# A recurrent cell's sigmoids, one to a batch, set behind the next step's decay copy, with some PSUM copies given to VectorE

## The chip, the cores and the metric

One core of a Trainium2 chip runs the kernel. Its engines work side by side, each on its own list of instructions: TensorE (PE; PEld is its weight loads), VectorE (DVE), ScalarE (ACT), GpSimd (POOL), and SyncE (SP), which here only issues transfers. Each engine takes its instructions in program order. The metric is the time of one execution on the device, in microseconds.

## The reference

Two blocks in a row. The first is a gated recurrence over 768 time steps, for 4 batches, 8 heads and a head width of 40; the second sends each of the 3072 resulting rows of 320 through one of 8 two-layer networks, chosen from a token number.

```python
for t in range(S):
    m_new = np.maximum(f_gate[:, :, t] + m, i_gate[:, :, t])
    f_stab = np.exp(f_gate[:, :, t] + m - m_new)
    i_stab = np.exp(i_gate[:, :, t] - m_new)
    C = f_stab * C + i_stab * (vt outer kt)
    n = f_stab * n + i_stab * kt
    h_tilde = C @ qt
    denom = np.maximum(np.abs(n . qt), 1.0)
    o = 1.0 / (1.0 + np.exp(-o_gate[:, :, t]))
    y[:, :, t] = o * h_tilde / denom
...
expert_idx = token_ids * 2654435761 % E
out[mask] = np.maximum(xe @ w1[e], 0.0) @ w2[e]
```

What the change is about is the line `o = ...`: a sigmoid over all elements of `o_gate`, 768 x 8 x 40 for each batch.

## The kernel before

**Stages.** The first stage (up to about 160 us of the profile) computes the recurrence in blocks of 128 time steps, as masked attention inside a block and a state `C` of 40 x 41 numbers per head carried from block to block. There are 6 blocks in a batch (`NB`), 4 batches, so 24 steps `s`, with `b = s // 6` and `c = s % 6`. The second stage gathers rows by expert and runs the networks on TensorE. All is Float32 with some BF16 helpers. The program order is written out by hand (`tc.manual_schedule()`): what a function issues goes to the end of each engine's list, and semaphores are put in where one engine reads what another wrote, or reuses a buffer.

**One step of the first stage**, in the order in which it is issued (L760 to L827):

- transfers for later steps on SP's queue (k, v, q, gate `og`, expert weights);
- `decayed` (L375): POOL multiplies the state by the decay `dec` copied in the step before;
- `turn_k` (L283): TensorE transposes k of step s+2, 128x512, into PSUM, and ScalarE copies it to `kT` (L289);
- `turn_q` (L295): the same for a block of q of the next batch, copied to `qT` (L302). For batches 1 to 3 the q rows are loaded six to a partition, so a block's columns are written with a step of 6 elements (`slice(r, None, NB)`);
- `back` and `finish` (L443, L451): the finished block of a batch before is transposed to `xo` in PSUM, VectorE forms the denominator `den`, multiplies by the gate `og`, POOL divides, and SP stores the rows;
- `decays` (L316): TensorE forms the log-decays `ab` of step s+1 in two halves, ScalarE takes their exponential into `w` (L328);
- in steps 3, 9 and 15, `load_e`: a transfer on ScalarE's queue (L203);
- in steps 5, 11 and 18, the sigmoids (L800), on `og` in place, 128x1920 for a batch;
- `state` (L386): TensorE forms k'v into the PSUM tile `ht`, VectorE adds it to the state `C`;
- `entering` (L330): for a step s+1 that is not the first of its batch, TensorE forms `xb`, VectorE multiplies it into `qs` (L340), and ScalarE copies the last column to `dec` (L342), the decay copy;
- `load_a` on SP, `k_weights` (L344) on POOL, and the stores of the finished rows on SP;
- `scores` (L359) of step s+1 on TensorE, then `weigh` (L370): VectorE multiplies the scores into `w` (L373, two instructions);
- `pad_q` (L291): VectorE spreads the q rows that the next step transposes; then in most steps some work of the routing tables (L648 to L655), on VectorE and POOL;
- `attend` (L404): TensorE forms the step's output in `ht`, and ScalarE copies it to `hB` (batches 0 to 2) or `hT` (batch 3) (L439);
- in steps 13 to 20, `route_table` (L623): a product on TensorE and two sums on VectorE (L631, L632).

**Buffers.** The PSUM tiles `tr`, `xo`, `ab`, `xb` and `tk` share one ring of four (`tag="tr", bufs=4`): each new one waits until the one four before it has been read. `ht` is a single buffer. `og` has three, so batch 3 takes the one of batch 0.

**ScalarE's tables.** Exponential and sigmoid need different tables; each change between them puts a load (ACT_TABLE_LOAD) into ScalarE's list, in front of the first instruction that needs it. Copies run with either.

**The place of the sigmoids.** Batch 0's is issued in step 5, those of batches 1 and 2 one after the other in step 11, batch 3's in step 18, each behind the exponentials of `decays(s + 1)` and ahead of `entering(s + 1)`. For steps 5 and 11 the next step is the first of a batch, so `entering` issues nothing there.

Of the kernel before, what the change touches and what calls it, by code (L numbers as in the profile page):

```python
# [17 lines left out]
P = 128  # L18
# [4 lines left out]
def kernel(  # L23
# [24 lines left out]
    nc = tc.nc  # L48
    B, H, S, D = q.shape
    BH = B * H  # L50
    NB = S // P
# [53 lines left out]
    def weight_slices(e):  # L105

        W[e], slices = weights(moe_w1[e], moe_w2[e], wpools[e % 3 > 0], w2pools[e % 6 > 0])
        return slices
# [8 lines left out]
    with tc.tile_pool(name="gates", bufs=1) as gp, \  # L117
# [35 lines left out]
        qb = {}  # L153
# [5 lines left out]
        def load_k(s):  # L159
            st[s] = {"k": ks[s % NK], "v": vs[s % NK]}  # L160
            nc.sync.dma_start(ks[s % NK][:, :, :D], rows_of(k, s))

        def load_v(s):
            nc.sync.dma_start(vs[s % NK][:, :, :D], rows_of(v, s))
# [5 lines left out]
        LB = B - 1  # L170

        def load_o(b, part):
            if part == 0:
                og[b] = ld.tile([P, H, NB * D], F32, name="og", bufs=3)
            if b == LB:
                nc.sync.dma_start(gate(b, part), rows_of(o_gate, b * NB + part))
                return
            hs = slice(part * PR, (part + 1) * PR)
            nc.sync.dma_start(og[b][:, hs], o_gate[b, hs].rearrange("h (p r) d -> p h (r d)", r=NB))
# [6 lines left out]
        def load_q(b, part):  # L186

            if part == 0:
                qb[b] = {"l": ld.tile([P, H, NB * D], F32, name="ql", bufs=2)}
            hs = slice(part * PR, (part + 1) * PR)  # L190
            nc.sync.dma_start(qb[b]["l"][:, hs], q[b, hs].rearrange("h (p r) d -> p h (r d)", r=NB))
# [80 lines left out]
        def gates_turn(rows):  # L272
# [7 lines left out]
                kw_T[:, :, lo:hi_, :].rearrange("p c g n -> p c (g n)"), tp[:],  # L280
            )

        def turn_k(s):  # L283
            d = st[s]
            d["kT"] = wk.tile([P, PR, P], F32, name="kT")
            tp = ps.tile([P, PR, P], F32, name="tr", tag="tr", bufs=4)
            for j in range(PR):
                nc.tensor.transpose(tp[:, j, :], d["k"][:, 2 * j : 2 * j + 2, :].rearrange("p h d -> p (h d)"), ident[:])
            nc.scalar.copy(d["kT"][:], tp[:])  # L289

        def pad_q(b, r):  # L291
            t = qb[b][r] = qps[(2 + r) % 4]
            nc.vector.tensor_copy(t[:, :, :D], qb[b]["l"][:, :, r * D : (r + 1) * D])

        def turn_q(b, r, cols):  # L295
            if "T" not in qb[b]:
                qb[b]["T"] = wk.tile([P, PR, S], F32, name="qT")
            t = qb[b].pop(r)
            tp = ps.tile([P, PR, P], F32, name="tr", tag="tr", bufs=4)
            for j in range(PR):  # L300
                nc.tensor.transpose(tp[:, j, :], t[:, 2 * j : 2 * j + 2, :].rearrange("p h d -> p (h d)"), ident[:])  # L301
            nc.scalar.copy(qb[b]["T"][:, :, cols], tp[:])  # L302


        def load_q0(c):
            t = qb.setdefault(0, {})[c] = qps[c % 2]
            nc.sync.dma_start(t[:, :, :D], rows_of(q, c))

        def turn_q0(c):
            turn_q(0, c, slice(c * P, (c + 1) * P))  # L310
# [33 lines left out]
        def k_weights(s):  # L344
            b, c = s // NB, s % NB
            d = st[s]
            if c + 1 < NB:
                d["kw"] = kws[s % 2]
                nc.gpsimd.tensor_tensor(
                    d["kw"][:, :, :D], d["k"][:, :, :D],  # L350
                    kw_T[:, c % 2, c // 2, b * H : (b + 1) * H].unsqueeze(2).to_broadcast([P, H, D]), op=ALU.mult,
                )
# [3 lines left out]
        def sigmoid(b):  # L356
            nc.scalar.activation(og[b][:], og[b][:], AF.Sigmoid)
# [17 lines left out]
        def decayed(s):  # L375
            c = s % NB
            if c == 0:
                st["C"] = None
            if c + 1 < NB:
                st["Cn"] = Cs[s % 2]  # L380
                if c > 0:
                    nc.gpsimd.tensor_tensor(
                        st["Cn"][:, :, :D1], st["C"][:, :, :D1], st[s]["dec"][:].to_broadcast([P, PR, D1]), op=ALU.mult,
                    )
# [19 lines left out]
        def attend(s):  # L404

            c = s % NB
            d = st[s]

            def place(j, hf):
                return d["ht"][j % 2 * DP : (j % 2 + 1) * DP, hf, j // 2 * P : (j // 2 + 1) * P]  # L410

            if c > 0:
                for j in range(PR):
                    for hf in range(2):
                        r = slice(hf * DP, (hf + 1) * DP)
                        nc.tensor.matmul(
                            place(j, hf), lhsT=st["C"][r, j, :], rhs=d["qs"][r, j, :],
                            start=(j < 2), stop=False, skip_group_check=True,
                        )
            for j0 in range(0, PR, 2):  # L420
                for hf in range(2):
                    for j in (j0, j0 + 1):
                        nc.tensor.matmul(  # L423
                            place(j, hf), lhsT=d["v"][:, 2 * j + hf, :], rhs=d["w"][:, hf, j, :],
                            start=(c == 0 and j0 == 0), stop=True,
                            skip_group_check=True,
                        )
            if c + 1 < NB:
                st["C"] = st["Cn"]
            b = s // NB  # L430
            if b == LB:
                hT[b, c] = wk.tile([P, 2, 2, P], F32, name="hT")[:]
                to = hT[b, c]
            else:
                if c == 0:
                    hB[b] = wk.tile([P, 2, 2, S], F32, name="hB")
                hT[b, c] = hB[b][:, :, :, c::NB]
                to = hB[b][:, :, :, c * P : (c + 1) * P]
            nc.scalar.copy(to, d["ht"][:, :, : 2 * P].rearrange("p f (i t) -> p f i t", t=P))  # L439

        hB, hT = {}, {}

# [317 lines left out]
        for s in range(NT):  # L760
            b, c = s // NB, s % NB
            if 0 < s < NT - 3:
                load_k(s + 3)
                if b == 0 and c < 3:
                    load_q0(c + 3)
            if s + 3 < NT:
                load_v(s + 3)
            if c in (2, 4) and b + 2 < B:
                load_q(b + 2, c // 2 - 1)
            for bo, part in o_loads.get(s, ()):  # L770
                load_o(bo, part)
            if s < 2:
                load_q(1, s)
            if s == NB + 4:
                slices += weight_slices(0)
            if slices:
                slices.pop(0)()
            decayed(s)
            if s + 2 < NT:
                turn_k(s + 2)  # L780
            if b == 0 and c < 4:
                turn_q0(c + 2)
            if b + 1 < B:
                for r in (turns_of if b else first_turns).get(c, ()):
                    turn_q(b + 1, r, slice(r, None, NB))
            done = [(b - 1, c)] if b > 0 else []
            if b == LB and c > 0:
                done.append((b, c - 1))
            stores = [finish(*br, back(*br)) for br in done]
            if s == 0:  # L790
                spin(5)
            if s + 1 < NT:
                decays(s + 1)
            if s == 0:
                store_a(g1, A)
                store_e(g1, A)
                store_e(g0, nc.sync)
            if c == 3 and b + 1 < B:
                load_e(b + 1, [0, 1, 2])
            for bo in {NB - 1: (0,), 2 * NB - 1: (1, 2), 3 * NB: (LB,)}.get(s, ()):  # L800
                sigmoid(bo)
            state(s)
            if s + 1 < NT:
                entering(s + 1)
                if 0 < s < NT - 2:
                    load_a(s + 2, nc.sync)
                if s == 0:
                    A.activation(aP[g1], aP[g1], AF.Exp)
                    load_a(2, A)
                    load_e(0, [1, 2])  # L810
                k_weights(s + 1)
            for store in stores:
                store()
            if s + 1 < NT:
                scores(s + 1)
                weigh(s + 1)
            nb = b + (c == NB - 1)
            if nb + 1 < B and s + 1 < NT:
                for r in (turns_of if nb else first_turns).get((c + 1) % NB, ()):
                    pad_q(nb + 1, r)  # L820
            for do in before.get(s, []):
                do()
            attend(s)
            if s == 0:
                gates_turn(g1)
            for do in after.get(s, []):
                do()  # L827
# [255 lines left out]
    with tc.manual_schedule():  # L1083
# [55 lines left out]
        for e in range(E):  # L1139
            g, i = e // EG, e % EG  # L1140
# [94 lines left out]
```

## Time and profile before

| | |
|---|---|
| median of 4 runs (lowest to highest) | 409.27 us (408.74 to 410.97) |
| the profiled execution: its time | 408.99 us |
| the profiled execution: its span | 407.2 us |
| first stage | until about 160 us |
| sigmoid, L357, 4 instructions | 7.1 us, 1802 ns each |
| table loads for sigmoid, L357, 3 | 1283 ns each |
| table loads for exponential behind them, L328, 3 | 1283 ns each |
| copies L439 (hB, hT), ACT, 24 | 14.0 us, 583 to 586 ns each |
| copies L289 (kT), ACT, 24 | 14.0 us, 585 ns each |
| copies L302 (qT), ACT, 24 | 22.6 us, 976 ns mean, 1099 ns median |
| products L373 (w), DVE, 48 | 30.9 us, 686 ns each |
| products L340 (qs), DVE, 20 | 13.6 us, 680 ns each |

The span runs from the first to the last instruction that the profiler shows; the execution's time has some 1.8 us around it. Times in a timeline are microseconds from the span's start: first the start of an instruction or a run of equal ones, then its length, engine, line, operation, tiles (written <- read), shapes, and in brackets the idle time ahead of it on its engine with what ended it. In the list of waits the numbers are total us, count, and the longest.

### The profile page before, as it was taken

What the parts mean: (1) busy time and instruction counts of PE and PEld (TensorE: products, weight loads), DVE (VectorE), ACT (ScalarE), POOL (GpSimd) and SP (SyncE); (2) the same over time, 40 slices, a digit from 0 to 9 for tenths busy, and PEclk for the clock granted to TensorE, in tenths of its full rate; (3) what the DMA queues carried; (4) which work ended last, traced back from release to release, by engine and by line L of the source; (5) the groups of instructions that cost most, each with busy time, mean ns of one, the idle gap of its engine ahead of it and who ended that gap; (6) DMA issues with size and microseconds to landing.
All of it is one profiled execution on the core that took longest, in us unless ns stands there. A gap on an engine that the chain in (4) does not pass through costs nothing. (4 is left out here: it accounts for less than half of the span.)

```text
span 407.2 us, 8799 instructions
## 1 busy us (share of the span) xinstructions
PE 382.2 (94%) x3406; PEld 313.5 (77%) x3406; DVE 213.5 (52%) x515; ACT 150.2 (37%) x290; POOL 200.6 (49%) x253
## 2 busy tenths in 40 slices
PE   8689989997999998999999999999999999999991
PEld 7568767875887775556998988977989989889771
DVE  7656647774786774235246347354345463452500
ACT  6334797579557541011114232241231141321300
POOL 6653103323544641784296395692592883907011
PEclk9959999999999999999999999999999999999998
DMA  7587856986678512447958137244236201000001
GB/s 143 110 191 160 209 110 153 238 200 132 150 170 184 143 48 81 104 165 224 336 205 257 66 99 225 82 113 147 88 106 183 81 2 47 2 15 34 0 17 35
DMA packets 96166, 51.47 MB, mean 126 GB/s; under 512 B 68022, under 2 KB 90170, under 8 KB 96122
## 3 DMA queue, kind: packets, MB, share of 16 engines
q1 hardware_dynamic: 88330, 36.65, 36.5%
q0 software_dynamic: 2496, 8.20, 6.3%
q10 hardware_dynamic: 5296, 6.03, 4.7%
q8 instruction: 28, 0.46, 0.5%
q14 instruction: 16, 0.13, 0.1%
HBM read 41.98 MB, written 8.63 MB: 124 GB/s over the span
## 5 line engine op out<-in xcount | busy, mean ns | idle before, releaser
L846 POOL DMA_INDIRECT out_dram<-zo,s_idx x26 | 27.2, 1046 | 89.7 <-DVE zo L1076 52.4
L465 POOL TENSOR_TENSOR x<-x,den 128x320 f32<-128x320 f32 x23 | 16.6, 722 | 50.7 <-DVE den L463 25.1
L373 DVE TENSOR_TENSOR w<-sp,w 128x512 f32<-128x512 f32 x48 | 30.9, 686 | 14.6 <-PE sp L365 12.9
L1038 PE MATMUL zp<-w2t,h 128*128 128x320 f32 x128 | 36.5, 438 | 0.0
L365 PE MATMUL sp<-qT,kT 64*128 64x128 f32 x384 | 29.4, 291 | 3.1 <-ACT qT L302 1.6
L1038 PEld LDWEIGHTS zp<-w2t,h 128*128 128x128 f32 x128 | 23.3, 190 | 11.4 <-issue 2.1
L365 PEld LDWEIGHTS sp<-qT,kT 64*128 64x128 f32 x384 | 24.6, 193 | 9.6 <-issue 4.5
L1008 ACT ACTIVATE h<-h 128x832 f32<-128x832 f32 x14 | 12.6, 897 | 47.6 <-DVE h L1007 47.6
L836 POOL DMA_INDIRECT xg<-x_rows,g_idx x24 | 23.3, 971 | 12.4 <-issue 12.4
L1048 PE MATMUL zp<-t,s 128*128 128x160 f32 x192 | 27.7, 300 | 1.3 <-DVE s L1033 0.6
L328 ACT ACTIVATE w<-ab 128x512 f32<-128x512 f32 x48 | 26.7, 611 | 5.8 <-PE ab L324 5.7
L1048 PEld LDWEIGHTS zp<-t,s 128*128 128x128 f32 x192 | 26.5, 190 | 1.7 <-ACT p L1062 0.9
L423 PE MATMUL ht<-w,v 128*64 128x128 f32 x384 | 27.1, 285 | 0.0
L1022 POOL TENSOR_TENSOR t<-w2t,t 128x640 f32<-128x640 f32 x16 | 24.7, 1543 | 0.6
L956 PE MATMUL mb<-xs,ws 128*128 128x208 f32 x112 | 25.0, 346 | 0.0
L1022 POOL TENSOR_TENSOR t<-w2t 128x640 f32<-128x640 f32 x16 | 24.8, 1551 | 0.1
L956 PE MATMUL ma<-xT,w1t 128*128 128x208 f32 x112 | 24.8, 346 | 0.0
L423 PEld LDWEIGHTS ht<-w,v 128*64 128x64 f32 x384 | 21.2, 140 | 4.0 <-issue 3.1
L302 ACT COPY qT<-tr 128x512 f32<-128x512 f32 x24 | 22.6, 976 | 0.8 <-PE tr L301 0.8
L956 PEld LDWEIGHTS mb<-xs,ws 128*128 128x128 f32 x112 | 19.6, 190 | 1.8 <-issue 1.5
L956 PEld LDWEIGHTS ma<-xT,w1t 128*128 128x128 f32 x112 | 18.9, 190 | 1.8 <-issue 1.8
L1048 PE MATMUL zp<-w2t,h 128*128 128x160 f32 x128 | 20.2, 301 | 0.0
(248 smaller groups left out, 864.8 us busy)
## 6 DMA issues: line engine op xcount, KB each, us to landing
w2t<-in_moe_w_dram SPq DMA_DIRECT2D x24, 320.0 KB
w1t<-in_moe_w_dram SPq DMA_DIRECT2D x24, 256.0 KB
k<-in_k_dram SPq DMA_DIRECT2D x24, 160.0 KB
v<-in_v_dram SPq DMA_DIRECT2D x24, 160.0 KB
x_rows<-x SPq DMA_DIRECT2D x24, 160.0 KB
ql<-in_q_dram SPq DMA_DIRECT2D x6, 480.0 KB
og<-in_o_gate_dram SPq DMA_DIRECT2D x6, 480.0 KB
w2t<-in_moe_w_dram ACTq DMA_DIRECT2D x8, 320.0 KB
```

Source lines behind the costliest of these rows:

```text
L302: nc.scalar.copy(qb[b]["T"][:, :, cols], tp[:])
L328: nc.scalar.activation(w[:, hf], ab[:], AF.Exp)
L365: nc.tensor.matmul(sp[hf][:, j, :], lhsT=d["kT"][r, j, :], rhs=q_of(s)[r, j, :], start=True, stop=True,)
L373: nc.vector.tensor_tensor(d["w"][:, hf], d["sp"][hf][:], d["w"][:, hf], op=ALU.mult)
L423: nc.tensor.matmul(place(j, hf), lhsT=d["v"][:, 2 * j + hf, :], rhs=d["w"][:, hf, j, :], start=(c == 0 and j0 == 0), stop=True, skip_group ...
L465: eng.tensor_tensor(xv, xv, den[:].to_broadcast([P, 2, PR, D]), op=ALU.mult)
L836: nc.gpsimd.indirect_dma_start(out=xg, out_offset=None, in_=x_d[:, :], in_offset=bass.IndirectOffsetOnAxis(ap=idx, axis=0),)
L846: ins = nc.gpsimd.indirect_dma_start(out=out[:, :], out_offset=bass.IndirectOffsetOnAxis(ap=idx, axis=0), in_=zo[:], in_offset=None, bound ...
L956: nc.tensor.matmul(dst[:, i, :], lhsT=x(2 * q + i), rhs=y, start=(start and i == 0), stop=stop, skip_group_check=True,)
L1022: nc.gpsimd.tensor_tensor(d[:], x, y[:] if y in (t1, t2) else y, op=ALU.subtract)
L1038: nc.tensor.matmul(zp[:], lhsT=h[:, fb, 2 * P : 3 * P], rhs=w2t[:, fb, :], start=(fb == 0), stop=(fb == FB - 1),)
L1048: nc.tensor.matmul(dst, lhsT=x[:, i], rhs=y[:, i], start=(start and i == 0), stop=(i == FB // 2 - 1), skip_group_check=True,)
```

## The change

The sigmoids are now issued behind `k_weights(s + 1)`, so behind `entering(s + 1)` with its decay copy, and each batch has a step of its own: 5, 11, 15 and 18 for batches 0 to 3. In those steps the copy L439 of `attend` is issued on VectorE in place of ScalarE, and in the steps after them (6, 12, 16, 19) the copies L289 and L302 of `turn_k` and `turn_q`. `turn_k(s)` is called with the step s+2, so it looks up `s - 3`; `turn_q` is given the step and looks up `s - 1`. The calls of `turn_q` for batch 0 keep ScalarE.

```diff
+        sig = {NB - 1: 0, 2 * NB - 1: 1, 2 * NB + 3: 2, 3 * NB: LB}
+
+        def from_psum(s):
+            return nc.vector.tensor_copy if s in sig else nc.scalar.copy
+
         def turn_k(s):
...
-            nc.scalar.copy(d["kT"][:], tp[:])
+            from_psum(s - 3)(d["kT"][:], tp[:])
...
-        def turn_q(b, r, cols):
+        def turn_q(b, r, cols, s=0):
...
-            nc.scalar.copy(qb[b]["T"][:, :, cols], tp[:])
+            from_psum(s - 1)(qb[b]["T"][:, :, cols], tp[:])
...
-            nc.scalar.copy(to, d["ht"][:, :, : 2 * P].rearrange("p f (i t) -> p f i t", t=P))
+            from_psum(s)(to, d["ht"][:, :, : 2 * P].rearrange("p f (i t) -> p f i t", t=P))
...
-                    turn_q(b + 1, r, slice(r, None, NB))
+                    turn_q(b + 1, r, slice(r, None, NB), s)
...
-            for bo in {NB - 1: (0,), 2 * NB - 1: (1, 2), 3 * NB: (LB,)}.get(s, ()):
-                sigmoid(bo)
             state(s)
             if s + 1 < NT:
                 entering(s + 1)
...
                 k_weights(s + 1)
+            if s in sig:
+                sigmoid(sig[s])
             for store in stores:
                 store()
```

## The prediction

> **What bounds the kernel now.** I read the engine shares first, then TensorE's waits, then the timeline around each sigmoid.
>
> ```profile
> span 407.2 us, 8799 instructions
> PE 382.2 (94%) x3406; PEld 313.5 (77%) x3406; DVE 213.5 (52%) x515; ACT 150.2 (37%) x290; POOL 200.6 (49%) x253
> PEclk9959999999999999999999999999999999999998
> ```
>
> TensorE (PE) is busy 94% of the span, at full granted clock from the fourth of the 40 slices on, so well before the first sigmoid at 56.8 us. Time can only come from the holes in its work. Its waits by releaser:
>
> ```profile
> PE xo L448 <- ACT hB L439: 3.1, 2, 2.4
> ...
> PE sp L365 <- ACT qT L302: 1.6, 3, 1.2
> ...
> PE xo L448 <- ACT hT L439: 1.4, 2, 0.7
> ...
> PE tr L301 <- DVE qp L293: 0.6, 2, 0.3
> ```
>
> The columns are total us, times, longest. The first row is two waits, 0.69 and 2.38 us, right behind the sigmoids of steps 5 and 11. Of the third, 0.64 us lies behind the sigmoid of step 18; the other, 0.74, is the last block's. The fourth is the two q transposes of the steps after the first two sigmoids. The second has nothing to do with a sigmoid. So what the change can touch is 0.69 + 2.38 + 0.64 + 0.6 = 4.3 us, and that is its ceiling. The timeline of ScalarE (start, length) at the dearest one, step 11, where two sigmoids run together:
>
> ```profile
> 88.89 1.28 ACT L357 ACT_TABLE_LOAD   x1
> 90.19 3.50 ACT L357 ACTIVATE og<-og 128x1920 f32<-128x1920 f32 x2
> 93.59 0.56 ACT L439 COPY hB<-ht 128x512 f32<-128x512 f32 x1
> 94.06 0.59 ACT L289 COPY kT<-tr 128x512 f32<-128x512 f32 x1
> 94.53 1.11 ACT L302 COPY qT<-tr 128x512 f32<-128x512 f32 x1
> 95.66 1.28 ACT L328 ACT_TABLE_LOAD   x1
> ```
>
> TensorE finished the attention output at 90.80, but its copy to hB waits for both sigmoids until 93.59; the transposes xo of step 12 start at 94.21. VectorE is idle meanwhile:
>
> ```profile
> 91.22 0.19 DVE L599 CAST rc<-rc_i 128x48 f32<-128x48 int32 x1
> 95.13 0.17 DVE L454 TENSOR_SCALAR den<-xo 128x8 f32<-128x8 f32 x1 [3.72 <-PE xo L448]
> ...
> 96.31 0.68 DVE L340 TENSOR_TENSOR qs<-qT,xb 128x512 f32<-128x512 f32 x1
> 97.58 1.29 DVE L373 TENSOR_TENSOR w<-sp,w 128x512 f32<-128x512 f32 x2 [0.59 <-ACT w L328]
> ```
>
> Behind the attention stage TensorE never waits 1 us, and the gathers, spins and weight loads there hang on the last step; what is won or lost before 160 us arrives at the end whole.
>
> **The change, part by part.** Steps 5, 11, 15 and 18 carry one sigmoid each; in each, the copy hB or hT (L439), and in the next step the copies kT (L289) and qT (L302; none in step 19), go from ScalarE to VectorE: 4 + 4 + 3 copies. Step 15 is new; its sigmoid costs one more pair of table loads.
>
> Durations. ScalarE: load 1.28, sigmoid 1.80, from the rows. Copies on VectorE have no row. hB and kT: the PSUM copy of 128x384 (L866) takes 557 ns, that of 128x164 (L400) 328 ns, so 1.04 ns an element and 0.69 us for 512, which is also what L340 and L373 take (680, 686). qT writes every sixth float: on ScalarE this raises 0.585 to 1.10 us. Bounds for VectorE: 0.69 (stride free) and 1.47 (the only strided vector row, the reduction L593, 623 ns for 192 elements against 329 ns for 168 in L558: 2.6 ns an element). I take 1.10, ScalarE's own row for this same write. Vector instructions follow each other about 0.08 before the printed end of the one before. A vector result reaches TensorE after 0.11 (pad L293 ends 63.98, load for L301 at 64.09).
>
> The ring matters: "tr" has four PSUM buffers. In a step they go to kT, qT, xo, ab, ab, xb, so the second ab waits for the kT copy and xb for the qT copy.
>
> *Step 11, sigmoid pair split.* VectorE is free at 91.33: hB 91.33 to 92.02, kT to 92.63, qT to 93.65. PE: xo at 92.13 (before 94.21), xb at 93.65 + 0.11 = 93.76 (95.84), scores(13) at 94.09 (96.17). Vector chain: den starts at 93.57, C 0.86 later (the four den instructions back to back, 60.74 to 61.60 in the next paragraph), qs 94.68; scores end at 95.25, weigh starts at 95.34 (97.58). ScalarE: sigmoid ends 91.99, load back 93.28, exponentials behind ab (93.5) in time. Weigh, pad, q transpose: all 2.24 earlier. **-2.24 us.**
>
> *Step 5, same sigmoid, copies moved.* VectorE has routing work until 58.58, so hB runs 58.50 to 59.19, hardly earlier than ScalarE had it (59.04). kT to 59.80, qT to 60.82; xb at 60.93 (60.72), scores 61.25 (61.04), ending 62.41. den starts at 60.74 instead of 59.94, C 61.60, qs 61.85, weigh 62.50 against 62.45, for it waited 0.59 for the exponential before. Pad and q transpose follow: **+0.05.** The stall has changed its owner.
>
> *Step 15, new.* ScalarE has nothing to do from the decay copy to the copy of hB:
>
> ```profile
> 113.74 0.16 ACT L342 COPY dec<-xb 128x4 f32<-128x4 f32 x1 [0.52 <-DVE qs L340]
> ...
> 115.59 0.59 ACT L439 COPY hB<-ht 128x512 f32<-128x512 f32 x1 [1.68 <-PE ht L423]
> ```
>
> Load, sigmoid, load: 113.90 + 1.28 + 1.80 + 1.28 = 118.3, so the next exponentials begin 0.6 later than their 117.69, ready at 119.4 for a weigh at 120.4. That cover holds, even if the load back were held until the first ab is written, at 117.6: exponentials until 120.1. VectorE is what gives: busy 5.71 of 7.40 us between 113.6 and 121, it gets 0.69 + 0.69 + 1.10 more. Its routing one-hot ends 116.23: hB 116.14 to 116.83, the two table sums until 117.18, kT 117.10 to 117.79, qT to 118.81. PE: ab at 117.29 and 117.90 (117.15 and 117.46), xb at 118.92 against 118.04. Scores 0.88 later; C, qs and weigh end at 120.49 against 119.62, 0.87. **+0.88** (qT at 0.69: +0.47; at 1.47: +1.25).
>
> *Step 18.* The decay copy no longer waits for the sigmoid (132.35 becomes 129.83), but nobody needed it sooner: the state product on POOL (L382, 132.83) stands behind other POOL work ending 132.86. hT: 132.13 to 132.82, 0.16 earlier than ScalarE. kT 133.09 to 133.78 now stands ahead of den, so the first xo is read by 134.46 and xb goes at 134.57 against 134.51: **+0.06.**
>
> The sigmoid issues no DMA; batch 3's input-piece load on ScalarE's own queue in step 15 (112.27) stays ahead of it, and nothing is moved on SP's or POOL's queue. The values of batch 2 are read first at 132.79, ready at 117.0.
>
> Sum: 0.05 - 2.24 + 0.88 + 0.06 = **-1.25 us**. With qT at 0.69: -1.7. At 1.47: step 5 +0.37, step 11 -1.9, step 15 +1.25, so -0.2. The profiled execution took 408.99 us (span 407.2), 0.28 under the median of 409.27; I put the difference on the median: **408.0 us**, forecast's own range 407.6 to 409.1.
>
> In the trace a load costs 1283 ns and the sigmoid starts 20 ns after it (88.89 + 1.28, then 90.19); no drain shows. The Trainium skill, "ScalarE: Activation LUTs" (What ACT_TABLE_LOAD costs; Rules for kernel authors), speaks against this change: do all of one set before switching, about 2.66 us a switch, 1.38 of it a drain. By that page step 15 would hold its exponentials until 121.0, weigh would come 1.2 us later still, and the sum would be about -0.1; the rows decide for 1.28.
>
> ScalarE's qT rows (0.585 flat, 1.10 at a step of 24 bytes) show that this write is dear. "SBUF — State Buffer" (the note on cachelines) says lines have 16 bytes and each access to a new line pays, without a price; by that page, if VectorE paid a whole second pass over 512 elements at the rows' 1.04 ns, an estimate of 0.69 + 0.53 = 1.22 us, the sum would be about -1.0.
>
> **The rivals.**
> A, *the stalls vanish whole*: 4.3 us off, 405.0. For it: VectorE idles 3.72 us at step 11. Against: it holds routing work at the three others, and has to take qT there too.
> B, *slower: the vector copies are stretched by GpSimd's work beside them.* The row for it is L1031, 692 ns at best, 1820 at worst, mean 1078 with POOL active: +0.39 an instruction. At that price eleven copies cost 4.2 us, -1.25 + 4.2 = +3.0, 412.2. It makes the kernel slower by 0.5% from 0.30 us a copy on. Against: POOL shows 12.06 us idle before 60.92 and 6.43 before 96.14, exactly where six of the copies fall, and L1031 reads SBUF, the copies PSUM.
> C, *VectorE does not catch up*: step 15's 0.88 is paid a second time in step 17, whose vector load is as high: -1.25 + 0.88 = -0.4, 408.9. Against: it idles 1.25 us a step there (0.68 + 0.37 + 0.20).
>
> **How the numbers follow.** Forecast 0.56, A 0.20, B 0.12, C 0.12. A measurement here can tell about 0.5%, 2.05 us, from no change. Faster by more: A and a little of the forecast's edge, 0.23. Slower by more: most of B, 0.11. Within: 0.66. The range goes from 406.8 (from the forecast's lower edge, 407.6, a third of the way to A) to 409.9 (C with qT at its dear end, 408.9 + 1.05). It leaves out most of B and half of A, 0.2.
>
> **What would show it.** Right: qT on VectorE near 1.1 us, and the times from scores to scores over the four places: 54.59 to 61.04, 88.02 to 96.17, 112.76 to 118.36 and 128.98 to 134.84 before, so 6.45, 8.15, 5.60 and 5.86, become about 6.7, 6.1, 6.5 and 5.9, with the intervals behind them not longer than before. Wrong: a vector copy over 1 us without a stride (B), or a second long interval behind step 16 (C), or a load back that starts only when ab is ready.

## The result, and the profile after

The changed kernel takes 408.3 us at the median (405.51 to 413.73) beside 409.08 us (407.03 to 414.01) for the kernel before, measured in turn on the same chips. The ratio is 0.9978, with a 95% interval of 0.9965 to 0.9992: a gain of 0.9 us, between 0.3 and 1.4. (The ratios leave out the few executions that took over 1.5% longer than the fastest of their kernel; the medians and ranges hold them.) Two more series of the changed kernel, on the chips of the experiments, gave 407.52 beside 409.38 (0.9958, 0.9928 to 0.9989) and 407.73 beside 409.79 (0.9961, 0.9943 to 0.9979). All three lie on the faster side, and all three gains are within what was called too small to tell from no change.

The head of the page of the changed kernel: the span, the busy time of each engine, and the clock that TensorE was granted in each of 40 slices.

```profile
span 406.0 us, 8793 instructions
PE 383.1 (94%) x3406; PEld 314.0 (77%) x3406; DVE 220.0 (54%) x526; ACT 146.6 (36%) x281; POOL 201.1 (50%) x253
PEclk9959999999999999999999999999999999999997
```

VectorE has eleven instructions more, the eleven copies, and 6.5 us more work; ScalarE has eleven copies less and one pair of table loads more. TensorE is as full as before. Its list of waits (total us, count, longest) shows who holds it now:

```profile
PE xo L454 <- DVE hB L445: 1.5, 2, 0.9
...
PE xo L454 <- DVE tv L637: 0.6, 1, 0.6
...
PE ab L330 <- DMA R<-decay_pieces: 0.4, 1, 0.4
...
PE ab L330 <- DVE kT L295: 0.2, 1, 0.2
```

The row of 3.1 us on ScalarE's hB is gone and one of 1.5 us on VectorE's hB stands in its place: the stall of step 5 changed its owner, 0.69 becoming 0.93, and that of step 11 went from 2.38 to 0.57. The second row is step 18, where hT now comes from VectorE (0.64 before, 0.56 now). The last row is new and belongs to step 15. The third is a wait for a transfer, far from any sigmoid; it comes back below. (Lines of the changed kernel are numbered six higher than those of the kernel before.)

The groups of VectorE's copies, with count, busy us and the mean ns of one:

```profile
L308 DVE COPY qT<-tr 128x512 f32<-128x512 f32 x3 | 3.2, 1079 | 0.0
...
L295 DVE COPY kT<-tr 128x512 f32<-128x512 f32 x4 | 2.7, 682 | 0.0
```

The best measure of each place is the time from one step's scores to the next step's on TensorE. The stretch behind a place is added, since a late vector chain can shift work into it. Here and below, the scores, the weigh or the interval of a step are those issued in it; since a step issues the scores of the next block, the scores of step 11 are those of block 12. Some of the recorded expectations count by the block ("the scores of step 12", "step 16") and mean the same instructions.

| place | before | after | difference | predicted |
|---|---|---|---|---|
| step 5 (two intervals) | 6.45 + 5.40 | 6.66 + 5.25 | +0.06 | +0.05 |
| step 11 (two intervals) | 8.15 + 5.39 | 6.41 + 5.25 | -1.88 | -2.24 |
| step 15 | 5.60 | 6.40 | +0.80 | +0.88 |
| step 18 | 5.86 | 5.85 | -0.01 | +0.06 |
| sum | | | -1.03 | -1.25 |

Outside the places, and behind the first three blocks, one more interval differs between these two profiles: from the scores of block 9 to those of block 10 (issued in steps 8 and 9), 5.49 before and 6.14 after, by the wait for the transfer. So the first stage ends only some 0.4 us earlier in the profile after, and the other 0.8 us of the difference between the two spans (407.2 and 406.0) arises behind it, where the two programs are the same: the stretch from the first product zp of the first expert to that of the second takes 27.57 in the one (188.57 to 216.14) and 26.87 in the other (188.13 to 215.00). That the spans differ by 1.2 and the sum was 1.25 is thus partly chance. The table, not the span, is the test of the prediction.

### The profile page after: what moved, and what is told of

Read it like the earlier page. It is cut to its first block, busy times and chain, and to the rows that moved or that the text cites. A ratio compares the mean times of both kernels' runs of the same rounds, so it can differ in the third digit from the quotient of the medians.

```text
span 406.0 us, 8793 instructions
## 1 busy us (share of the span) xinstructions
PE 383.1 (94%) x3406; PEld 314.0 (77%) x3406; DVE 220.0 (54%) x526; ACT 146.6 (36%) x281; POOL 201.1 (50%) x253
## 5 line engine op out<-in xcount | busy, mean ns | idle before, releaser
L1044 PEld LDWEIGHTS zp<-w2t,h 128*128 128x128 f32 x128 | 23.3, 190 | 11.4 <-issue 2.1
L1054 PEld LDWEIGHTS zp<-w2t,h 128*128 128x128 f32 x128 | 18.5, 190 | 2.0 <-issue 1.0
```

The lines of the kernel that those rows point to most:

```text
L1044: nc.tensor.matmul(zp[:], lhsT=h[:, fb, 2 * P : 3 * P], rhs=w2t[:, fb, :], start=(fb == 0), stop=(fb == FB - 1),)
L1054: nc.tensor.matmul(dst, lhsT=x[:, i], rhs=y[:, i], start=(start and i == 0), stop=(i == FB // 2 - 1), skip_group_check=True,)
```

## The experiments

**Sigmoids one to a batch, all copies left on ScalarE.** Which half of the change does the work in step 11, the split of the pair or VectorE's copies?

Against the changed kernel:

```diff
         def from_psum(s):
-            return nc.vector.tensor_copy if s in sig else nc.scalar.copy
+            return nc.scalar.copy
```

> One sigmoid per batch in steps 5, 11, 15, 18 behind the decay copy, all copies left on ScalarE. Theory (VectorE's copies are what makes the fourth sigmoid bearable): step 5 unchanged, step 11 -1.65 us (one sigmoid of 1.80 less ahead of the copies, the exponentials still last), step 15 +1.0 (copies behind the sigmoid, then the load back), step 18 +0.6 (the sigmoid ends 0.6 later than before because the decay copy goes first): sum near 0, ratio 0.999 to 1.001. Rival (the split alone makes the gain): as the changed kernel, ratio 0.998 or below.

Measured: 408.19 us beside 409.38, ratio 0.9977 (0.995 to 1.0004), unclear. The intervals are 6.46 in step 5, 6.46 in step 11 (-1.69), 6.59 in step 15 (+0.99) and 6.53 in step 18 (+0.67): they add up to nothing. The split alone wins nearly what the whole change wins in step 11, and loses it in steps 15 and 18. The median is lower by 1.2 us all the same, so the intervals of one profile do not tell the whole; the hole in step 12 is 0.69 here, and what a long hole does to the clock comes below.

**The pair kept in step 11, VectorE's copies there, and nothing in step 15.** Against the changed kernel:

```diff
-        sig = {NB - 1: 0, 2 * NB - 1: 1, 2 * NB + 3: 2, 3 * NB: LB}
+        sig = {NB - 1: (0,), 2 * NB - 1: (1, 2), 3 * NB: (LB,)}
...
-            if s in sig:
-                sigmoid(sig[s])
+            for bo in sig.get(s, ()):
+                sigmoid(bo)
```

> The two sigmoids of step 11 stay together, nothing in step 15; the copies of steps 5, 11 and 18 (and of the steps behind them) on VectorE. Theory (the copies waiting behind the sigmoids were the stall, not the sigmoids' length): step 5 +0.05, step 11 -2.0 (now held by the exponentials: second sigmoid ends 93.7, load back 95.0, first half 95.6, 0.25 later than VectorE would be ready), step 15 nothing, step 18 +0.06: -1.9 us, ratio 0.9945 to 0.9965, 0.6 to 0.9 us better than the changed kernel. Rival (the split is what pays): the pair keeps the exponentials and so the weighing of step 12 late, step 11 gains under 0.7 us, ratio 0.998 to 1.0.

Measured: 406.81 us beside 409.38, ratio 0.9938 (0.9913 to 0.9963). Step 11 takes 6.42 + 5.24, the same as with the pair split; step 15 is back at 5.60; step 18 is 5.84. ScalarE's timeline of this kernel at step 11 (start, length) and VectorE's beside it:

```profile
89.87 3.50 ACT L363 ACTIVATE og<-og 128x1920 f32<-128x1920 f32 x2
93.39 1.28 ACT L334 ACT_TABLE_LOAD   x1
94.68 1.08 ACT L334 ACTIVATE w<-ab 128x512 f32<-128x512 f32 x2
```

```profile
91.36 0.68 DVE L445 COPY hB<-ht 128x512 f32<-128x512 f32 x1
91.96 0.68 DVE L295 COPY kT<-tr 128x512 f32<-128x512 f32 x1
92.56 1.10 DVE L308 COPY qT<-tr 128x512 f32<-128x512 f32 x1
...
95.38 1.29 DVE L379 TENSOR_TENSOR w<-sp,w 128x512 f32<-128x512 f32 x2 [0.20 <-PE sp L371]
```

With the three copies on VectorE, ScalarE runs both sigmoids until 93.37 and nobody waits: the first of two exponentials that take 1.08 together, from 94.68, is ready for a weigh at 95.38 that the scores release. The split and the copies are two cures for the same stall. Each is enough alone (-1.69 and -1.73 on the interval, -1.74 for both), so the split bought nothing more and cost 0.80 in step 15.

**Old steps and the old pair, only the new place behind the decay copy.** Against the changed kernel (the loop over `sig` as in the experiment before):

```diff
-        sig = {NB - 1: 0, 2 * NB - 1: 1, 2 * NB + 3: 2, 3 * NB: LB}
+        sig = {NB - 1: (0,), 2 * NB - 1: (1, 2), 3 * NB: (LB,)}
...
-            return nc.vector.tensor_copy if s in sig else nc.scalar.copy
+            return nc.scalar.copy
```

> The sigmoids in their old steps, two in step 11, all copies on ScalarE; only their place in the step is the new one, behind the decay copy. For steps 5 and 11 this leaves every engine's order of work as it was. Theory 1 (the wait for a decay piece in the interval of the scores of step 9 to 10, 5.59 to 6.39 us instead of 5.49 in six of six profiles with the new place and routing work in its old one, comes from the new place): above 5.55 again. Rival (it comes and goes with the execution): 5.49. Step 18: the sigmoid ends 0.6 later than before, so the interval behind it is 6.5 instead of 5.86, as in e1_split_only; step 11 keeps its hole, 8.15 or, with a fall of the clock behind it, 8.6 to 9.2. Ratio 1.0005 to 1.004.

Measured: 410.16 us beside 409.11, ratio 1.0034 (0.9993 to 1.0075), unclear. Step 18 takes 6.52 instead of 5.86, as in the first experiment. TensorE's timeline of this kernel at steps 12 and 19:

```profile
93.45 0.81 PE L454 MATMUL xo<-ident,hB 128*128 128x128 f32 x4 [2.38 <-ACT hB L445]
...
96.12 2.02 PE L371 MATMUL sp<-qT,kT 64*128 64x128 f32 x16
```

```profile
134.37 0.65 PE L454 MATMUL xo<-ident,hT 128*128 128x128 f32 x4 [1.30 <-ACT hT L445]
```

The hole of 2.38 us is what it was before: in step 11 there is no decay copy to go behind, so the place changes nothing there. In step 18 the sigmoid now starts later, and a ScalarE copy behind it holds the transposes for 1.30 us, 0.66 more than before. So the new place by itself can only lose, and what makes it free in the changed kernel is VectorE's copy. (The scores of 2.02 us, elsewhere 1.16, are a matter of the clock, below.) The interval from block 9 to block 10 is 5.49 in this profile: the place alone does not bring the wait for the transfer, and the theory that it does was wrong.

**Step 15: its copies without its sigmoid.** The sigmoids as before the change; only the copies of steps 15 and 16 on VectorE. Against the changed kernel (the sigmoids' call is back in its old place):

```diff
-            return nc.vector.tensor_copy if s in sig else nc.scalar.copy
+            return nc.vector.tensor_copy if s == 2 * NB + 3 else nc.scalar.copy
```

> The kernel before, its sigmoids where they were, with only the three copies around step 15 (hB of step 15, kT and qT of step 16) on VectorE. Theory (step 15's price in the changed kernel is VectorE's copies, the sigmoid runs in ScalarE's idle time): the interval after the scores of step 16, 5.60 in the kernel before and 6.40 in the changed one, is 6.3 to 6.45 here too; all other intervals as in the kernel before. Rival (the sigmoid and its loads are the price): 5.60 to 5.75.

Measured, in one execution (409.54 us): the interval of step 15 is 6.40, exactly the changed kernel's, with no sigmoid near. VectorE and TensorE there:

```profile
116.67 0.68 DVE L444 COPY hB<-ht 128x512 f32<-128x512 f32 x1
117.27 0.19 DVE L636 TENSOR_TENSOR tv<-tv,tk 128x47 f32<-128x47 f32 x1
117.49 0.20 DVE L637 TENSOR_TENSOR tv<-tv,tk 128x47 f32<-128x47 f32 x1
117.61 0.68 DVE L294 COPY kT<-tr 128x512 f32<-128x512 f32 x1
118.22 1.07 DVE L307 COPY qT<-tr 128x512 f32<-128x512 f32 x1
119.14 0.15 DVE L459 TENSOR_SCALAR den<-xo 128x8 f32<-128x8 f32 x1
```

```profile
118.35 0.41 PE L329 MATMUL ab<-R,L 128*64 128x512 bf16 x2 [0.19 <-DVE kT L294]
...
119.34 0.41 PE L341 MATMUL xb<-R,Lx 128*64 128x512 bf16 x2
```

The vector list has no gap from the first copy on, and xb comes 0.05 behind the end of the qT copy (118.22 + 1.07 = 119.29). In this execution the price of step 15 is VectorE's, to the last hundredth. It is no way out to leave the copies on ScalarE: then the sigmoid holds them, and the first experiment paid 0.99.

**The changed kernel with the strided qT of step 16 back on ScalarE.** If the 1.08 us of that one copy made half of the price, this would halve it.

```diff
-            from_psum(s - 1)(qb[b]["T"][:, :, cols], tp[:])
+            (nc.scalar.copy if s == 2 * NB + 4 else from_psum(s - 1))(qb[b]["T"][:, :, cols], tp[:])
```

> The changed kernel, with the strided copy qT of step 16 back on ScalarE, behind the sigmoid and ahead of the load back. Theory (the strided write on VectorE is half of what step 15 costs): ScalarE ends the sigmoid at 117.0, qT at 118.1 instead of VectorE's 118.8, then the load back until 119.4, exponentials from 119.4, first half 120.0: the interval after the scores of step 16, 6.40, becomes 6.0, the rest as in the changed kernel: ratio 0.994 to 0.997. Rival (ScalarE's exponentials then come last): interval 6.4 or above, ratio as the changed kernel or worse.

Measured: 407.4 us beside 410.1, ratio 0.9956 (0.9936 to 0.9976); the interval of step 15 is 6.29, not the 6.0 that was expected. TensorE in this kernel:

```profile
115.02 0.41 PE L330 MATMUL ab<-R,L 128*64 128x512 bf16 x2 [0.41 <-ACT qT L308]
115.23 0.64 PE L402 MATMUL ht<-v,kw 128*64 128x41 f32 x16
115.67 0.42 PE L342 MATMUL xb<-R,Lx 128*64 128x512 bf16 x2
```

ScalarE takes the copy only behind the sigmoid, at 113.91, and ends it at 114.97, 0.23 behind VectorE's kT. The second half of ab now waits 0.41 for that, where the changed kernel waited 0.19 for kT. One wait took the other's place, and 0.11 is what is left of the gain. That theory, half of the price in one stride, was wrong.

**Three idle writes ahead of the weigh.** In step 11 the changed kernel fell 0.36 short of the sum, and the starts of the single instructions show where: from the scores of step 11 to its weigh it is 1.62 us in every kernel with the vector copies of step 6 and the routing work in its old place, and 1.26 in those without the copies. Before, after, and the kernel of this experiment, which is the kernel before with three writes to a tile that nobody reads, issued on VectorE in step 6 (VectorE's timelines at the weigh of step 11):

```diff
+            if s == NB:
+                more = gp.tile([P, 1], F32, name="more")
+                for _ in range(3):
+                    nc.vector.memset(more[:], 0.0)
```

> The kernel before, with three tiny writes to an unread tile on VectorE in step 6, where the changed kernel has its three more copies; nothing moved. Theory (the weighing of step 11 starts 0.36 us late in every kernel with vector copies because of where it then stands in VectorE's list of instructions): it begins 1.62 us after the start of the scores of step 12, as there. Rival (the copies themselves make it late): 1.26 us after, as in the kernel before. All else as before, 6.45, 8.15, 5.60, 5.86.

```profile
89.28 1.29 DVE L373 TENSOR_TENSOR w<-sp,w 128x512 f32<-128x512 f32 x2 [1.10 <-PE sp L365]
```

```profile
90.35 1.29 DVE L379 TENSOR_TENSOR w<-sp,w 128x512 f32<-128x512 f32 x2 [1.44 <-PE sp L371]
```

```profile
94.24 1.29 DVE L373 TENSOR_TENSOR w<-sp,w 128x512 f32<-128x512 f32 x2 [1.45 <-PE sp L365]
```

The scores of step 11 start at 88.02, 88.73 and 92.62 in the three, so the weigh comes 1.26, 1.62 and 1.62 behind. Nothing was moved to VectorE in the third, and none of the three writes is near step 11: three instructions more in VectorE's list are enough, be they copies or idle writes. The brackets name TensorE as the releaser, but its scores take 1.16 us in all three. (This one execution took 414.26 us; its first steps were already 5 us late, ahead of the edit.) Why they delay this one instruction is open. An 8 KB transfer of instructions lies near this spot, but in these traces it begins about a microsecond behind the late weigh (the weigh at 90.35 and 94.24, the transfer from 91.5 and 95.0 on). In each of the six profiles with this late weigh, it begins 0.07 to 0.09 us ahead of the end of GpSimd's product `kw`; in those with 1.26 it begins in the middle of that product. Whether the product holds it was not tried.

**The pair and the vector copies, with the routing work of steps 5 and 11 ahead of the weigh.** If in both steps the copy hB waits for routing work on VectorE, issuing that work earlier, where VectorE waits for the scores anyway, should win both. Against the kernel of the pair and the vector copies:

```diff
                 scores(s + 1)
+                if s in (NB - 1, 2 * NB - 1):
+                    for do in before.pop(s):
+                        do()
                 weigh(s + 1)
```

> The pair kept in step 11, vector copies in steps 5, 11 and 18, and VectorE's routing work of steps 5 and 11 issued ahead of the weighing instead of behind it, into VectorE's idle time there (4.1 and 1.1 us in the first profile). Theory (what stood between TensorE and the copy hB was routing work on VectorE): in step 5 hB starts at 57.5 instead of 58.5, the interval of the scores 6.66 becomes about 5.75, 0.9 us; step 11 stays held by the exponentials behind the second sigmoid, so 0.0 to 0.2 more: -2.8 us against the kernel before, ratio 0.992 to 0.9945. Rival (VectorE is full, the routing work is paid wherever it stands): intervals as without it, 6.66 and 6.42, ratio 0.994 to 0.996.

Measured: 405.38 us beside 410.1, ratio 0.9896 (0.9872 to 0.9921), from six executions. A second series of the same kernel:

> The kernel of e5_pair_route again, beside the changed kernel on one chip. Theory: by its intervals (5.60 + 5.24 instead of 6.45 + 5.40 behind step 5, 5.84 + 5.75 instead of 8.15 + 5.39 behind step 11) it does 3.0 us less than the kernel before and 2.0 less than the changed kernel; ratio 0.990 to 0.9945. Rival (the 0.9896 of its first six runs was the chip's): 0.996 or above, the changed kernel within 0.002 of it.

406.01 us beside 409.79, ratio 0.9933 (0.9906 to 0.9959), while the changed kernel in the same series took 407.73. VectorE at step 11 in this second series:

```profile
87.46 0.72 DVE L604 TENSOR_SCALAR rc_i<-sl_i 128x24 int32<-128x24 int32 x1
88.21 0.66 DVE L605 CAST rc<-rc_i 128x48 f32<-128x48 int32 x1
88.79 1.27 DVE L379 TENSOR_TENSOR w<-sp,w 128x512 f32<-128x512 f32 x2
...
94.73 1.29 DVE L379 TENSOR_TENSOR w<-sp,w 128x512 f32<-128x512 f32 x2 [0.68 <-ACT w L334]
```

The intervals are 5.60 + 5.25 in step 5 (-1.00 against before) and 5.85 + 5.75 in step 11 (-1.94), step 18 as before. In step 5 the stall is gone whole. In step 11 the next limit shows: with the copies done early, the weigh of step 12 waits for the exponentials behind the second sigmoid, 0.68 us, and the following interval gives back 0.36. Two tiny routing instructions take 0.72 and 0.66 us here, where they took 0.17 and 0.19 before. In their new place they run beside two products of GpSimd (POOL), and each ends just behind one of them. The first series has the same picture; this is its timeline, GpSimd's lines with VectorE's:

```profile
87.66 0.72 POOL L471 TENSOR_TENSOR x<-x,den 128x320 f32<-128x320 f32 x1 [4.83 <-PE ab L330]
87.69 0.72 DVE L604 TENSOR_SCALAR rc_i<-sl_i 128x24 int32<-128x24 int32 x1
...
88.34 0.72 POOL L355 TENSOR_TENSOR kw<-k,kw_T 128x320 f32<-128x320 f32 x1
...
88.45 0.66 DVE L605 CAST rc<-rc_i 128x48 f32<-128x48 int32 x1
```

The ends are 88.38 and 88.41, then 89.06 and 89.11. In the kernel before GpSimd was idle while these two ran (its products ended at 89.71, they started at 91.02 and 91.22). So the weigh of step 11 is late here too (1.66 and 1.67 behind its scores), but behind these two instructions. This is the fastest version found, and it differs from the proposed change in having no split.

**The clock behind the hole: the kernel before, and the changed one, once more.**

> The kernel before against itself, for the noise of one comparison and for a second trace. Theory: ratio 1.000 with an interval of some 0.1 to 0.2%; steps of 6.45, 8.15, 5.60 and 5.86 us from scores to scores at the four places again; the stretch from 160 us to the end may differ by up to 1 us between executions, as the changed kernel's first profile has it 0.7 us shorter there with the same instructions. Rival (this stretch got shorter through the change): within 0.2 us of the first profile of the kernel before.

Measured beside itself: 408.77 and 409.38 us, ratio 1.0008 (0.9982 to 1.0034), as it should be. But its profile shows 9.17 + 5.76 at step 11 where the first profile of the same program had 8.15 + 5.39. The stretches of that profile: the window, its length, the busy us of TensorE (with the number of instructions), then PEld, DVE, ACT and POOL, the granted clock, and the transfers' share and GB/s.

```profile
95.10:98.50 3.40, 1.02 (x8) 0.72 (x5) 0.00 (x0) 3.40 (x5) 0.00 (x0) 1.00 0.92 183
98.55:101.90 3.35, 3.35 (x33) 2.45 (x34) 1.87 (x6) 3.22 (x5) 1.40 (x2) 0.50 0.19 56
101.95:105.35 3.40, 3.24 (x38) 2.62 (x34) 2.20 (x5) 1.60 (x3) 0.94 (x2) 1.00 0.47 81
```

Behind the 2.38-us hole TensorE was granted half its clock for some 3.4 us, and the two intervals together took 1.39 us longer. In the changed kernel the hole is 0.57. The repetitions of the changed kernel:

> The changed kernel a second time. Theory (my sum of the steps holds, what deviates is the execution's own): steps from scores to scores at the four places again near 6.7, 6.1 to 6.4, 6.4 and 5.9 us; the interval of 6.14 us from the scores of step 9 to those of step 10 in the first profile (a decay-piece transfer landed late, 0.65 us) goes back to 5.5, and the 0.37 us by which the weighing of step 11 began late goes away; ratio to the kernel before 0.996 to 0.999. Rival (the changed VectorE order causes both): 6.14 and the late weighing stand there again, ratio not below 0.998.

> The changed kernel a third time, on the same chip. Theory: sum of its intervals -1.0 us against the kernel before, and somewhat more in the median because the hole that lowers the clock is gone: ratio 0.9955 to 0.9985; intervals 6.66, 6.41, 6.41, 5.85 at the four places. Rival (no gain): 0.999 or above.

Their times stand above; their intervals at the four places agree with the table to 0.02. Neither shows a half clock at step 12. The first of the two theories was half wrong: the weigh of step 11 is late by the same 0.36 in both, and the interval from block 9 to block 10 takes 5.88 and 6.39. Both come with the change, not with one execution; the ratio was below the rival's 0.998 nevertheless.

**The hole filled with idle products.** The kernel before, with nine products of the identity into a scores tile in step 12's hole.

```diff
+            if s == 2 * NB:
+                fill = ps.tile([P, PR, P], F32, name="sp0")
+                for _ in range(9):
+                    nc.tensor.matmul(fill[:, 0, :], lhsT=ident[:], rhs=ident[:], start=True, stop=True)
```

> The kernel before, with 9 matmuls of the identity (2.1 us, their result is not read) in TensorE's hole in step 12, nothing else. Theory (the hole of 2.4 us makes the granted clock fall to half for a window of 3.4 us in part of the executions, as in the second profile of the kernel before, where the two intervals behind it were 9.17 and 5.76 instead of 8.15 and 5.39, 1.4 us): the interval stays 8.15, no window of half clock near 100 us, mean granted clock over the runs 0.983 to 0.985 as in the changed kernels instead of 0.981, time 0.5 to 1.0 us lower, ratio 0.997 to 0.999. Rival (the clock falls for another reason): mean clock 0.981, ratio 1.000 or above.

Measured: 409.67 us beside 410.1, ratio 0.9984 (0.996 to 1.0008), unclear. The products run 2.17 us and leave a wait of 0.38; the intervals stay at 8.14 + 5.41, and no half clock shows. The mean granted clock over the executions is 0.9835 (12), beside 0.9813 for the kernel before in the same series (22). The clock went the expected way, by about twice the error of that difference; a gain in time is within the interval, but not shown.

## Why the prediction was right, and where it was off

**What sets the end.** Right. The change won in TensorE's holes around the sigmoids, and no other engine became the bound. From the last scores of the first stage to the end of the span it is 254.4 to 255.4 us in thirteen of the fourteen profiles, with and without the change (256.1 in the one with a half clock there), so what is won ahead arrives at the end on the mean, though one execution can hide it. The prediction overlooked one wait of 1.02 us at the start of the second stage (before the product at 160.07; at 159.68 after): it is the same in both.

**Durations.** hB and kT were taken as 0.69 and measured 0.683 and 0.682; qT was taken as 1.10 and measured 1.079. ScalarE's row for the strided write was the right neighbour, which was a guess that held: nothing here shows why the two engines need the same time for it. The flat price (0.69) and the strided reduction (1.47) were both far off. The estimate from "SBUF — State Buffer" (the note on cachelines), 1.22, was above the measured copy. The sigmoid starts 20 ns behind its load in the new place too (112.74 + 1.28, then 114.04), and no load shows the drain of 1.38 us that "ScalarE: Activation LUTs" (What ACT_TABLE_LOAD costs) states: here the measurement decides against the page.

**Step 5.** Right, to the instruction. These are VectorE and TensorE of the changed kernel; hB was predicted for 58.50, xb for 60.93, scores for 61.25, weigh for 62.50.

```profile
58.52 0.68 DVE L445 COPY hB<-ht 128x512 f32<-128x512 f32 x1
...
60.95 0.39 PE L342 MATMUL xb<-R,Lx 128*64 128x512 bf16 x2
...
61.27 1.16 PE L371 MATMUL sp<-qT,kT 64*128 64x128 f32 x16
...
62.53 1.29 DVE L379 TENSOR_TENSOR w<-sp,w 128x512 f32<-128x512 f32 x2 [0.19 <-PE sp L371]
```

**Step 11.** The mechanism was right and one term mis-sized: "VectorE is free at 91.33" was read from the trace of before, 3.31 us behind the scores of step 11. In the changed kernel hB starts 3.66 behind them (92.39 - 88.73), because the weigh and all that follows it come 0.36 later. VectorE and TensorE of the changed kernel there:

```profile
92.39 0.68 DVE L445 COPY hB<-ht 128x512 f32<-128x512 f32 x1
...
93.22 0.78 PE L454 MATMUL xo<-ident,hB 128*128 128x128 f32 x4 [0.57 <-DVE hB L445]
```

The rest of the step keeps its predicted spacing: the three copies follow at 0.60 each, and TensorE starts xo 0.83 behind the start of hB (0.80 predicted). So -2.24 became -1.88, and the three idle writes show, in one execution, that the 0.36 comes with three more instructions in VectorE's list and not from the copies' work.

**Step 15.** Right: +0.80 against +0.88, by the cause that was named. The cover on ScalarE held as worked out, since the load back ran directly behind the sigmoid. These are ScalarE's lines of the changed kernel, and VectorE's weigh:

```profile
114.04 1.81 ACT L363 ACTIVATE og<-og 128x1920 f32<-128x1920 f32 x1
115.87 1.28 ACT L334 ACT_TABLE_LOAD   x1
117.16 1.09 ACT L334 ACTIVATE w<-ab 128x512 f32<-128x512 f32 x2
```

```profile
116.52 1.08 DVE L308 COPY qT<-tr 128x512 f32<-128x512 f32 x1
...
119.24 1.29 DVE L379 TENSOR_TENSOR w<-sp,w 128x512 f32<-128x512 f32 x2
```

The exponentials end at 118.25, a microsecond ahead of their reader. Step 18: -0.01 against +0.06.

**The rivals.** A, the stalls vanish whole, did not come: VectorE's routing work holds hB in step 5, and step 15 pays. The version with the routing work ahead shows for step 5 that this was the reason. B, copies stretched by GpSimd: none is above 0.69 without a stride. The copy hB of step 15 ran from 114.96 to 115.64 beside a GpSimd product (114.72 to 115.69) and took its usual 0.68. What GpSimd did stretch, in the version with the routing work ahead, were two small instructions and no copy. C, a second payment in step 17: the intervals behind step 16 are 5.20 and 5.42, as before.

**The sum and the median.** The median is 408.3 where 408.0 was forecast, inside the range of 406.8 to 409.9. The places give -1.03 for -1.25. Two things that no step had lie beside them. One is the wait for the decay pieces between the scores of blocks 9 and 10, 0.4 to 0.9 us in the three profiles of the changed kernel. The other is the half clock behind the hole, a loss of the kernel before that its shown profile happened not to have. The first takes from the gain, the second adds to it. That the measured gain (0.9 in the comparison of the change, 1.9 and 2.1 between the medians of the two repetitions) is near the sum is the balance of these and no proof of any one term.

**Open.** The wait for the decay pieces: the interval from block 9 to block 10 is 5.49 or 5.50 in all profiles of the kernel before and of those made from it with old sigmoid places, 6.14, 5.88 and 6.39 in the changed kernel, 5.98 with ScalarE's copies only, 5.89 with one qT moved back, 5.59 with the pair; but 5.49 with the place alone, and 5.49 and 5.50 with the routing work ahead. SP issues the same transfers in the same order in all. So neither the place nor the copies alone make it, as far as one profile of each can say; that it is a matter of when transfers meet was not tried.

## What to carry to other kernels

Two cures for one stall do not add: try each alone, and keep the one that costs nothing elsewhere; here moving three copies to an idle engine made the split of the sigmoids needless. When work is given to an engine in a place where it is idle, look first for what stands ahead of it in that engine's own list, for there the new wait arises, and moving that work can be worth as much as the change itself. Price a step from its own intervals in the trace, not from the difference of two spans.

## What the runs showed of the hardware

**A hole of 2.3 us can halve the clock.** Five profiles have the full hole at step 12 (before, its repetition, the idle writes, the copies of step 15 alone, the new place alone). In four of them a half clock of some 3.4 us follows, and the two intervals take 1.26 to 1.44 us longer than in the fifth; in the eight profiles with the hole shortened and in the one with it filled, there is none at that place. One profile of the changed kernel has such a window elsewhere, behind the waits of 0.74 and 1.02 us at the start of the second stage (granted clock 0.56 from 159.55 to 162.95), and from there to the first product zp it takes 1.5 us longer than in the first profile of the changed kernel; the first profiles of both kernels have the same two waits without it. So whether a hole does it differs between executions, and what decides was not found. The hole in step 12 lies between transposes: in the repetition of the kernel before, TensorE runs nothing else from 94.35 to 98.57, 4.2 us, and in the changed kernel from 91.44 to 93.93, 2.5 us. Whether transposes count as work for the clock was not tried; the filling was products of another kind. Over all executions the mean granted clock goes along: 0.9783 to 0.9813 in six series with the hole, 0.982 to 0.9848 in nine without it; beside the kernel before on the same chip it is about 0.002 higher. A difference of 0.002 is 0.002 x 407 / 0.5 = 1.6 us of half clock in an execution, as an estimate, so about 0.8 us of time on the mean. The Trainium skill, "TensorE: Matmul & The Clock Gate" (HAM oscillation — how this bites in real kernels), warns of idle gaps above about 3.4 us; here 2.28 us was enough (the kernel with the idle writes), in a stretch of 3.4 us in which TensorE still worked for 1.02 (the repetition of the kernel before).

**Three more instructions in VectorE's list can cost 0.36 us.** Three tiny writes five steps ahead delayed an instruction that mattered, in one execution; by what is open. **Small VectorE instructions can be held by GpSimd's products beside them**: two that took 0.17 and 0.19 us with GpSimd idle took 0.72 and 0.66 when started beside a product of 0.72, each ending 0.03 to 0.05 behind a product, in both profiles of that kernel. **A copy from PSUM on VectorE** costs 0.68 us for 128x512 floats, 0.10 more than on ScalarE, and 1.08 to 1.10 with a step of 24 bytes, about what ScalarE takes (1.10).
